# The decay row of a chunk pair through a small transfer and one product of eight rows; no xr where ot stands on GpSimd

## The chip, the cores and the metric

The kernel runs on one core of one Trainium2 chip. Its metric is the device time of an execution in microseconds (us). The core has five engines with an instruction queue each: TensorE (PE; its weight loads are listed apart as PEld), VectorE (DVE), ScalarE (ACT), GpSimd (POOL) and SyncE (SP), which here issues nearly all transfers. An instruction waits, at the head of its engine's queue, for the semaphores of the others.

## The reference

Inputs are `q`, `k`, `v`, `a_re`, `a_im` of shape (4, 8, 768, 48), batch, heads, steps, head width, and the weights of a layer behind. For every batch and head a complex state of 48 x 48 is carried over the steps, and its result goes through a normalised two-layer net:

```python
mag = sqrt(a_re**2 + a_im**2); scale = minimum(mag, 0.999) / (mag + 1e-6)
...
for t in range(S):                  # per batch and head, S complex, 48 x 48
    S = a[t][:, None] * S + outer(k[t], v[t])
    y[t] = q[t] @ real(S)
...
x = y as (B, S, 384)                # heads side by side
mu, var = mean(x), mean((x - mu)**2)
xn = (x - mu) / sqrt(var + 1e-6) * g_ln
out = x + maximum(xn @ w_ch1, 0) @ w_ch2      # 384 -> 1536 -> 384
```

## The kernel before, in words

The 768 steps of a batch are six chunks of 128 steps, taken in pairs: a pair P (0 to 11, three per batch) has the chunks n = 2P and 2P + 1. The recurrence is unrolled inside a pair. With the running product of the decays, written as `e` (magnitude of the product up to a step, `en` its inverse) and `trig` (cosine and sine of its angle), the keys become `ks` and the queries `qs`: the magnitudes go in as `ke = k * en` and `qe = q * e`, the angles as two halves of 64 columns per head, cosine and sine (48 used, the rest is zero padding). Then `am` is the 128 x 128 product of keys and queries per head, `atm` its masked form, `y` the result from `atm` and `v` and from the state `G` of the chunk before, and `gm` the product of `ks` and `v` that is added to the state. At the end of a pair the state is multiplied, row by row, by the magnitude of the decay over the whole pair (L668 and L673, operand `dec`): this is the step that the change is about. Behind `y` come the statistics `bn` (into `mv`, mean and variance), `x`, which is the mean less y, its transposed form `xT`, the net `mm1`, `relu`, `mm2`, and `ot`, the result, which `st` stores.

How the decay over a pair gets to its place: `e` of the pair has steps in partitions and (head, width) along the free axis. Wanted is the last step's row, 8 heads x 48, with the width in partitions and the heads along the free axis. `dps` (L577) does it on TensorE with eight products, one per head: the weights are the 128 x 48 block of `e` of that head, and the moving operand is the last column of the identity, one column wide, so that each product picks out the last row. `decc` (L585) copies the 48 x 8 result from PSUM twice into the tile `dec`, into partitions 0 to 47 and 64 to 111. The tiles `dec` are set to zero at the start by `zdec` (L352). Pairs 2, 5, 8 and 11 are the last of their batch and have no carry, so eight pairs have a `dps`: 0, 1, 3, 4, 6, 7, 9, 10.

How `ot` comes about: it is y + rstd * o, with o from `mm2` in PSUM. `xr` (L708) is -x + mean, which is y again, in 32 bits. On VectorE `ot` is a single operation on o, rstd and xr. GpSimd reads nothing from PSUM in this kernel, so where `ot` stands on GpSimd (chunks 2, 14, 15, 17, 18, 19, 20) ScalarE first writes rstd * o (`oa`, L781), and GpSimd adds xr (L789).

Order: there is no scheduler at build time. A plan written out, the text `PLAN` (L42 to L141), names every step once with its engine (P, A, V, G, S), and for TensorE's results the PSUM bank; on each engine the steps are issued in the order of the text. A step that writes into a tile of a ring (`RINGS`, L25) waits for those that used the tile last. `@name` puts a GpSimd step behind another. SP's queue is one such order too: loads, stores, transposes by transfer (`ksT`, `qsT`, `xT` on S) and the new step all stand in one line, and every transfer uses the next of eight completion semaphores, so that it also waits for the eighth before it. The `warm` steps are products without a use, which run on TensorE while the first loads come in. The weights `w1b` and `w2b` are loaded by GpSimd's own queue (`wl.0`, `wl.1`), `wl.0` behind `qs.0.0.0` on VectorE.

Lines of the profile that come up: L484 `dec` sums ahead of `e`; L488 `e`, `en`; L499 and L503 `ph` (the angles); L521, L532, L544 sine and cosine; L528 `qt`, which turns the angles a quarter; L579 `dps`; L598 transposes of `ks` and `qs`; L621 `am`; L645 `gm`; L682 and L685 `y`; L719 `xtr`, the transposes of x; L752 `mm1`; L776 `mm2`; L764 and L766 `relu`; L806 and L810 `warm`; L448 and L452 loads of a_re and a_im; L400 loads of q, k, v; L370 the small load `gln`; L603 and L725 transposes by transfer; L797 stores. L287, L289 and L292 are helpers that many steps share (copies on ScalarE and VectorE, and products of two tiles).

Of the kernel before, what the change touches and what calls it, by code (L numbers as in the profile page):

```python
# [50 lines left out]
ln.2.0:A car.1.0:V2 q.1.1:S warm.w26:P1 warm.w27:P1 warm.5:P1 warm.6:P1 dec.0.1:P1 lc.0.0:V l.1.0:V en.0.1:A1
warm.7:P4 dec.0.0:P7 e.0.1:A1 iv.2.0:A q.1.0:S lc.1.0:V qe.0.1.0:V warm.w28:P4 warm.w29:P4 warm.8:P4 warm.9:P4
warm.10:P4 dec.1.0:P4 en.0.0:A7 uthc:V vf.0.0:S e.0.0:A7 r.2.0:V e.1.0:A4 warm.11:P1 warm.12:P1 dps.0:P7 are.3.0:S
r2.2.0:V en.1.0:A4 ke.0.0.0:V u.2.0:A gln:S ke.0.1.0:V qe.0.0.0:V aim.3.0:S qe.1.0.1:V qe.1.0.0:V k.1.0:S l.2.0:V
tab.trig.3:A sin.0.0:A6 sin.0.1:A0 warm.w30:P1 warm.w31:P1 warm.w32:P1 warm.w33:P1 warm.13:P1 warm.14:P1@en.1.0
warm.w34:P1 warm.w35:P1 warm.w36:P1 warm.w37:P1 warm.15:P1 warm.16:P1@qe.0.0.0 warm.w38:P1 warm.w39:P1 warm.w40:P1
warm.17:P1 warm.18:P1 warm.19:P1 warm.20:P1 qt.0.0:P6 qs.0.0.1:V sin.1.0:A2 qt.0.1:P0 ks.0.0.1:V vf.1.1:S lc.2.0:V
cos.0.0:A6 ks.0.1.1:V warm.21:P1 warm.22:P1 qt.1.0:P2 qs.1.0.1:V cos.0.1:A0 vf.1.0:S dps.1:P5 qs.0.1.1:V cos.1.0:A2
dec.2.0:P0 ks.0.1.0:V k.2.1:S ks.0.0.0:V decc.0:A7 qs.0.1.0:V kT.0:P6 decc.1:A5 qs.0.0.0:V th.2.0:A qs.1.0.0:V
wl.0:G@qs.0.0.0 qT.0:P2 q.2.1:S v.0:V qT.1:P3 ksT.0:A6 qsT.0:V2 qT.2:P4 ke.1.0.0:G@v.0 k.2.0:S kT.1:P5 qsT.1:A3  # L60
qsT.2:V4 am.0:P6 ke.1.0.1:G@v.0 ksT.1:V5 gm.0:P4 atm.0:V6 ks.1.0.1:G warm.23:P2 warm.24:P2 am.1:P2 qT.3:P5 tab.log.4:A
ln.3.0:A atm.1:V2 y.0:P6 ks.1.0.0:G G.0:A4 e.2.0:A0 warm.w41:P7 warm.25:P7 warm.26:P7 warm.27:P7 gm.1:P4 bn.0:V6
ph.2.0:P2 iv.3.0:A qsT.3:V5 one:G kT.2:P7 x.0:A6 G.1:V4 r.3.0:G en.2.0:A0 ksT.2:V7 warm.28:P5 xtr.0:P6 kT.3:P4 xT.0:V6
am.2:P0 ksT.3:V4 y.1:P5 v.1:G atm.2:V0 am.3:P6 tab.trig.5:A th.3.0:A xr.0:G gm.2:P4 bn.1:V5 ngl:G sin.2.0:A2 r2.3.0:G
ph.3.0:P0 atm.3:V6 x.1:A5 q.2.0:S car.3.0:A0 y.2:P5 G.2:V4 sin.3.0:A0 xtr.1:P7 qt.2.0:P2 are.4.0:S wc.1.1:V gm.3:P4
xT.1:A7 wc.1.0:V qt.3.0:P0 wc.1.2:V cos.2.0:A2 wl.1:G@xT.1 vf.2.0:S wc.0.0:V mm1.0.1.0:P6 wc.0.1:V cos.3.0:A0 bn.2:V5
y.3:P3 aim.4.0:S mm1.0.1.1:P6 wc.0.2:V x.2:A5 wc.2.1:V wc.2.2:V mm1.0.0.1:P0 wc.2.0:V relu.0.1:A6 bn.3:V3
qe.2.0.1:G@wc.2.0 xtr.2:P2 mm1.0.0.0:P0 xT.2:V2 x.3:V3 ke.2.0.1:G@wc.2.0 mm1.0.2.1:P6 gs.3:V4 xtr.3:P2 mm1.0.2.0:P6
rstd.1:G xT.3:V2 tab.log.6:A u.3.0:A ke.2.0.0:V mm1.1.0.1:P2 relu.0.0:A0 l.3.0:V mm1.1.1.0:P4 relu.0.2:A6 mm1.1.1.1:P4
ks.2.0.0:V lc.3.0:V mm1.1.2.1:P0 ks.2.0.1:V relu.1.1:A4 qe.2.0.0:V dec.3.0:P6 rstd.0:A qs.2.0.0:V mm1.1.0.0:P2  # L70
en.3.0:A6 qs.2.0.1:V kT.5:P4 vf.2.1:S e.3.0:A6 qT.4:P5 mm1.1.2.0:P0 ksT.5:A4 qsT.4:V5 qT.5:P6 are.5.0:S G.3:V
relu.1.2:A0 kT.4:P5 qsT.5:V6 mm2.0.0:P4 are.6.0:S ksT.4:V5 ln.4.0:A am.5:P6 mm2.0.1:P4 iv.4.0:A atm.5:V6 aim.5.0:S
mm2.0.2:P4 relu.1.0:A2 am.4:P0 r.4.0:V q.3.0:S mm2.1.0:P5 atm.4:V0 r2.4.0:A v.2:G@r.4.0 mm2.1.1:P5 q.3.1:S mm2.1.2:P5
xr.2:G@r.4.0 u.4.0:A ot.0:V4 mm2.2.0:P6 ln.5.0:A l.4.0:V st.0:S gm.4:P2 mm2.2.1:P6 iv.5.0:A G.4:V2 y.4:P0 lc.4.0:V
ln.6.0:A mm2.2.2:P6 xr.3:V k.3.0:S bn.4:V0 xr.1:G@xr.3 dec.4.0:P2 iv.6.0:A r.5.0:G@xr.3 k.3.1:S x.4:V0 y.5:P1 e.4.0:A2
dps.3:P4 bn.5:V1 xtr.4:P0 vf.3.1:S mm2.3.0:P7 oa.2:A6 xT.4:V0 en.4.0:A2 vf.3.0:S x.5:V1 mm2.3.1:P7 qe.3.0.0:G ot.1:V5
r2.5.0:A xtr.5:P0 k.4.1:S mm2.3.2:P7 rstd.2:G xT.5:V0 qe.3.0.1:V mm1.2.0.0:P0 u.5.0:A aim.6.0:S qs.3.0.0:V
mm1.2.0.1:P0 qs.3.0.1:V q.4.1:S mm1.2.2.1:P2 ke.3.0.0:V ot.3:V7 mm1.2.2.0:P2 k.4.0:S tab.trig.7:A th.4.0:A ke.3.0.1:V
qT.6:P5 relu.2.2:A2 ks.3.0.0:V ph.4.0:P6 q.4.0:S decc.3:V4 ks.3.0.1:V relu.2.0:A0 mm1.2.1.0:P2 l.5.0:V k.5.0:S kT.7:P4
abs.4.0:A6 qsT.6:V5 v.3:G@l.5.0 dps.4:P1 car.4.0:A6 kT.6:P0 vf.4.0:S ksT.7:V4 sin.4.0:A6 r.6.0:G@l.5.0 qT.7:P5  # L80
ksT.6:V0 mm1.2.1.1:P2 are.8.0:S decc.4:A1 qsT.7:V5 th.5.0:A am.6:P6 st.1:S gm.6:P4 relu.2.1:A2 ot.2:G ph.5.0:P0
atm.6:V6 are.7.0:S th.6.0:A ke.4.0.0:G am.7:P2 G.6:V4 y.6:P5 sin.5.0:A0 mm2.5.0:P6 atm.7:V2 ke.4.0.1:G vf.4.1:S
cos.4.0:A mm2.5.1:P6 qe.4.0.1:G bn.6:V5 mm2.5.2:P6 abs.5.0:A0 q.5.0:S ks.4.0.1:V y.7:P2 cos.5.0:A q.5.1:S lc.5.0:V
gm.7:P4 mm2.4.0:P7 ks.4.0.0:V x.6:A5 bn.7:V2 mm2.4.1:P7 xr.5:G@ks.4.0.0 r2.6.0:A aim.7.0:S G.7:V4 qe.4.0.0:G@ks.4.0.0
mm2.4.2:P7 x.7:V2 k.7.0:S dec.5.0:P0 qs.4.0.0:V xtr.6:P2 qs.4.0.1:V xtr.7:P3 st.2:S kT.9:P4 tab.log.8:A e.5.0:A0
# [5 lines left out]
u.7.0:A xr.6:G@qs.5.0.0 vf.5.0:S abs.6.0:V0 r.8.0:G@qs.5.0.0 y.9:P4 y.8:P2 k.6.1:S bn.9:V4 mm2.7.0:P3 q.7.1:S bn.8:V2
gm.9:P7 tab.trig.9:A sin.6.0:A0 mm2.7.1:P3 ke.5.0.1:G gs.9:V7 are.9.0:S x.9:A4 mm2.7.2:P3 ot.6:V6 ke.5.0.0:G th.7.0:A
qT.11:P4 x.8:V2 st.6:S dps.6:P5 G.9:G cos.6.0:A car.6.0:V0 qT.10:P2 q.6.0:S qsT.11:V4 xtr.8:P6 ke.6.0.0:G xtr.9:P7
ph.7.0:P0 xT.8:A6 xT.9:V7 th.8.0:A qsT.10:V2 q.6.1:S mm1.4.1.1:P6 l.7.0:V decc.6:A5 car.7.0:A0 mm1.4.0.1:P4 abs.7.0:A0
ks.5.0.0:V mm1.4.0.0:P4 r2.8.0:V aim.9.0:S sin.7.0:A0 ks.5.0.1:V mm1.4.1.0:P6 relu.4.0:A4 lc.7.0:V kT.10:P1 ot.7:V3
q.7.0:S ke.6.0.1:G@lc.7.0 kT.11:P2 relu.4.1:A6 ksT.10:V1 k.7.1:S mm1.4.2.0:P4 ksT.11:V2 st.5:S am.10:P0 ks.6.0.1:V
am.11:P6 atm.10:V0 dec.7.0:P2 v.5:G@ks.6.0.1 tab.log.10:A rstd.4:A mm1.4.2.1:P4 ln.9.0:A vf.6.0:S xr.8:G@ks.6.0.1
atm.11:V6 y.10:P0 qe.6.0.0:G e.7.0:A2 mm2.9.0:P1 k.8.0:S bn.10:V0 en.7.0:A2 qe.6.0.1:G ph.8.0:P6 q.8.1:S relu.4.2:V4
u.8.0:A ks.6.0.0:G mm2.9.1:P1 are.11.0:S iv.9.0:A gm.10:P2 mm2.9.2:P1 G.10:V2 abs.8.0:A6 mm2.8.0:P3 qs.6.0.0:V x.10:A0
# [747 lines left out]
```

## Time and profile before

| | |
|---|---|
| three runs | 186.82, 187.60, 187.69 us |
| span of the profiled execution | 185.6 us |
| TensorE busy | 177.0 us (95%), 2029 products |
| VectorE, ScalarE, GpSimd busy | 157.7, 154.6, 99.8 us (85, 83, 54%) |
| moved by transfers | 35.34 MB, mean 190 GB/s |
| clock that TensorE was granted | full, mean 1.000 |

The span is the time from the first to the last instruction; the runs' times lie somewhat above it. Busy time is a sum over the whole execution. Where it matters what a step is worth, the place of the step counts: whether the chain of waits, which follows the last instruction back to what released it, runs over its engine there. In a row of the timeline the first number is the start in us from the span's start, the second the length, then engine, line, operation, result and operands. Products on TensorE overlap, so one's length is more than its share of time; the distance from one start to the next is the share. "SPq" marks the issuing of a transfer by SP, not the transfer.

### The profile page before, as it was taken

Reading aid. Unit: us, or ns where it says so; the run is one execution under the profiler, and the core shown is the slowest. Engines: PE = TensorE matmul, PEld = TensorE weight load, DVE = VectorE, ACT = ScalarE, POOL = GpSimd, SP = SyncE. Lnnn points to the kernel's source line nnn. Section 1 sums busy time; section 2 is a strip of 40 time slices with the busy share of each in tenths; the row PEclk is TensorE's granted clock in tenths of the full one; section 3 lists DMA queues with packets and bytes.
Section 4 is the critical chain, followed back from the end, with each engine's and each line's share of the span. In section 5 each row is a group of like instructions: output and inputs, shape, how many; then the busy total and the mean of one; then the engine's idle time right before and its main releaser. Section 6 shows DMA issues by size and latency. Waiting matters only on the chain.

```text
span 185.6 us, 5131 instructions
## 1 busy us (share of the span) xinstructions
PE 177.0 (95%) x2029; PEld 139.0 (75%) x2029; DVE 157.7 (85%) x302; ACT 154.6 (83%) x218; POOL 99.8 (54%) x128
## 2 busy tenths in 40 slices
...
GB/s 154 309 229 206 246 199 191 206 143 189 262 187 213 226 228 230 212 273 181 222 238 151 168 150 241 190 227 200 183 159 139 246 147 202 163 193 73 70 82 87
DMA packets 128440, 35.34 MB, mean 190 GB/s; under 512 B 124448, under 2 KB 127648, under 8 KB 128416
## 3 DMA queue, kind: packets, MB, share of 16 engines
...
q8 instruction: 16, 0.26, 0.6%
...
## 4 chain that ended last, share of the span: by engine, by line
PE 59%; ACT 14%; DMA 10%; DVE 10%; issue 3%; SPq 2%; DVEq 0%
PE banks L752 22%; PE banks L776 19%; DMA w1b<-in_moe_w_ch_dram 7%; PE banks L598 4%; PE banks L621 4%; ACT L815 3%; PE banks L484 2%; DMA are<-in_a_re_dram 2%; DMA k<-in_k_dram 2%; ACT are L457 2%; PE banks L682 2%; DVE l L473 1%; ACT h L764 1%; PE banks L685 1%; ACT w L455 1%
## 5 line engine op out<-in xcount | busy, mean ns | idle before, releaser
L752 PE MATMUL banks<-xT,w1b 128*128 128x256 bf16 x432 | 52.7, 273 | 0.2
L776 PE MATMUL banks<-w2b,h 128*128 128x384 bf16 (+2 forms) x300 | 52.5, 319 | 0.0
L752 PEld LDWEIGHTS <-w1b 128*128 128x128 bf16 x432 | 45.8, 114 | 1.7 <-DVE w1b L381 0.4
L764 ACT ACTIVATE h<-banks 128x1024 bf16<-128x1024 f32 x33 | 32.8, 1022 | 8.3 <-PE banks L752 8.1
L776 PEld LDWEIGHTS <-h 128*128 128x128 bf16 x300 | 26.9, 97 | 14.1
L292 DVE TENSOR_TENSOR atm<-banks,mask 128x1024 bf16<-128x1024 f32 x24 | 28.9, 1218 | 1.9 <-PE banks L621 1.6
L815 ACT ACT_TABLE_LOAD x15 | 19.2, 1283 | 1.0 <-PEq L831 0.8
L292 POOL TENSOR_TENSOR ke<-k,en 128x384 bf16<-128x384 f32 x14 | 12.7, 916 | 8.3 <-DVE l L476 5.6
L292 POOL TENSOR_TENSOR qe<-q,e 128x384 bf16<-128x384 f32 x15 | 13.7, 916 | 6.1 <-DVE w1b L381 1.9
L292 POOL TENSOR_TENSOR ks<-ke,trig 128x768 bf16<-128x768 bf16 x7 | 11.4, 1643 | 6.4 <-PE banks L752 4.2
L621 PE MATMUL banks<-qsT,ksT 128*128 128x128 bf16 x192 | 14.6, 219 | 0.1
L410 POOL TENSOR_SCALAR v<-vf 128x768 bf16<-128x768 f32 x7 | 5.8, 831 | 16.0 <-DVE r L292 8.9
L810 PE MATMUL banks<-u_e 128*128 128x512 f16 x42 | 11.7, 418 | 2.2 <-POOL u_e L320 2.2
L292 POOL TENSOR_TENSOR r<-aim,are 128x768 f16<-128x768 f32 x7 | 12.7, 1817 | 1.9 <-ACT x L699 1.5
L709 POOL TENSOR_SCALAR xr<-x,mv 128x384 f32<-128x384 bf16 x16 | 9.3, 586 | 8.1 <-PE banks L752 3.3
L621 PEld LDWEIGHTS <-ksT 128*128 128x128 bf16 x192 | 12.0, 98 | 1.8 <-DVE ksT L289 0.5
L692 DVE BATCH_NORM_STATS2 stats<-banks 128x6 f32<-128x384 f32 x24 | 13.4, 556 | 0.1
L682 PE MATMUL banks<-v,atm 128*128 128x48 bf16 x192 | 12.1, 183 | 0.3 <-ACT x L699 0.2
L473 DVE SCALAR_TENSOR_TENSOR l<-r,w 128x768 f16<-128x768 f16 (+1 forms) x13 | 11.5, 892 | 0.9 <-ACT r L469 0.7
L791 DVE SCALAR_TENSOR_TENSOR ot<-banks,rstd,xr 128x384 f32<-128x384 f32 (+2 forms) x18 | 10.5, 590 | 2.0 <-PE banks L776 1.6
L455 ACT ACTIVATE w<-are 128x768 f32<-128x768 f32 (+1 forms) x13 | 10.2, 790 | 2.3 <-DMA are<-in_a_re_dram 2.3
L682 PEld LDWEIGHTS <-atm 128*128 128x128 bf16 x192 | 11.0, 96 | 1.2 <-DVE atm L292 0.2
...
## 6 DMA issues: line engine op xcount, KB each, us to landing
k<-in_k_dram SPq DMA_DIRECT2D x24, 192.0 KB, 4.1
q<-in_q_dram SPq DMA_DIRECT2D x24, 192.0 KB, 4.2
vf<-in_v_dram SPq DMA_DIRECT2D x24, 192.0 KB, 4.0
out_dram<-ot SPq DMA_DIRECT2D x23, 192.0 KB, 3.4
are<-in_a_re_dram SPq DMA_DIRECT2D x8, 384.0 KB, 4.7
aim<-in_a_im_dram SPq DMA_DIRECT2D x8, 384.0 KB, 4.8
are<-in_a_re_dram SPq DMA_DIRECT2D x8, 192.0 KB, 3.7
aim<-in_a_im_dram SPq DMA_DIRECT2D x8, 192.0 KB, 3.8
```

The source lines that it names most:

```text
L292: {"DVE": nc.vector, "POOL": nc.gpsimd}[eng(name)].tensor_tensor(**kw)
L455: add(f"ln.{X}", lambda S_=S_: act(out=S_("w"), in_=S_("are"), func=AF.Ln), needs=[f"are.{X}"], uses=[("are", P), ("w", P)])
L473: nc.vector.scalar_tensor_tensor(out=S_("l"), in0=S_("r2"), scalar=0.5, in1=S_("w"), op0=ALU.mult, op1=ALU.add)
L621: nc.tensor.matmul(ps[:, h], lhsT=T("ksT", n)[:, h], rhs=T("qsT", n)[:, h], start=True, stop=True)
L682: nc.tensor.matmul(ps[:, h], lhsT=T("atm", n)[:, h], rhs=T("v", P)[:, c, h], start=True, stop=nfirst)
L692: nc.vector.bn_stats(out=T("stats", n), in_=bank(f"y.{n}")[:, 0:DM])
L752: nc.tensor.matmul(ps[:, jj], lhsT=w1b[:, dc, ts(gi, JG * C)].rearrange("k (p j) -> k j p", j=JG)[:, jj], rhs=T("xT", P)[:, dc].rearrange( ...
L764: act(out=dst, in_=src, func=AF.Relu)
L776: nc.tensor.matmul(bank(f"o.{N}")[:, ws], lhsT=T("h", P)[:, j, ts(c, C)], rhs=w2b[:, j, ws], start=(j == 0), stop=(j == NJ - 1))
L791: nc.vector.scalar_tensor_tensor(out=o, in0=bank(f"o.{N}")[:, ws], scalar=T("rstd", P)[:, ds(c, 1)], in1=xs, op0=ALU.mult, op1=ALU.add)
L810: g.add(f"warm.w{i}", lambda i=i: nc.tensor.matmul(bank(f"warm.w{i}"), lhsT=u_e[:, 0, 0], rhs=u_e.rearrange("p c j t -> p (c j t)"), start ...
L815: g.add(f"tab.{nm}.{i}", lambda tab=tab: nc.scalar.preload_act_table_set(tab))
```

## The change

It does three things. `dps` becomes two steps. `row` is a transfer issued by SP: it takes the last row of `e`, which lies in one partition, and writes its eight stretches of 48 numbers (96 bytes) into eight partitions of a new small tile of 64 columns, whose last 16 columns stay zero (`zrow`, two GpSimd memsets in place of the three of `zdec`). `dps` is then a single product: weights are that tile, 8 rows by 64 columns, the moving operand is the 8 x 8 identity, and the result has 64 rows by 8. `decc` copies 64 rows instead of 48, so that `dec` needs no zeros of its own.

Where `ot` stands on GpSimd, `xr` isn't made any more: `oa` adds the mean along with the scaling, and GpSimd subtracts x. Seven `xr` go, those of chunks 2, 15, 17, 19, 20 on GpSimd and 14, 18 on VectorE.

The plan has the new steps. Every step that stays keeps its engine and its place among the steps of its engine, with two exceptions on TensorE: `dps.0` stands later, behind the warm-up product `warm.w40`, and `dps.10` stands behind `xtr.15` and `ph.10.0`, where it stood ahead of both. The eight `row` steps stand in SP's queue: `row.0` behind `gln`, `row.1` behind `aim.3.0`, `row.3` behind `q.3.0`, `row.4` behind `aim.6.0`, `row.6` behind `q.7.1` and ahead of `are.9.0`, `row.7` behind `are.11.0`, `row.9` behind `q.10.0`, `row.10` behind `k.9.0` and ahead of the transposes `ksT.17` and `qsT.17`. The code for `ke`, `qe`, `ks` and `qs` also gets a form in one operation for both halves; the plan names both halves everywhere, so that form isn't used.

```diff
-            def f_dps():
-                for h in range(H):
-                    nc.tensor.matmul(bank(f"dps.{P}")[0:D, ds(h, 1)],
-                                     lhsT=T("e", P)[:, R - 1, ts(h, D)],
-                                     rhs=ident[:, C - 1:C], start=True, stop=True)
-            add(f"dps.{P}", f_dps, needs=[f"e.{P}.{i}" for i in range(NS)] + ["ident"],
-                uses=[("e", P)], ps=(f"dps.{P}", 1))
-
-            def f_decc():
-                for a in range(2):
-                    put(f"decc.{P}", T("dec", P)[ds(a * HALF, D)], bank(f"dps.{P}")[0:D, 0:H])
-            add(f"decc.{P}", f_decc, needs=[f"dps.{P}", "zdec"], uses=[("dec", P)],
-                ps=(f"dps.{P}", 1))
+            add(f"row.{P}", lambda: nc.sync.dma_start(
+                out=T("row", P)[0:H, 0:D].unsqueeze(1),
+                in_=T("e", P)[C - 1:C, R - 1].rearrange("p (h d) -> p h d", d=D)),
+                needs=[f"e.{P}.{i}" for i in range(NS)] + [f"zrow.{P % RINGS['row']}"],
+                uses=[("e", P), ("row", P)])
+            add(f"dps.{P}", lambda: nc.tensor.matmul(
+                bank(f"dps.{P}")[0:HALF, 0:H], lhsT=T("row", P)[0:H], rhs=ident[0:H, 0:H],
+                start=True, stop=True),
+                needs=[f"row.{P}", "ident"], uses=[("row", P)], ps=(f"dps.{P}", 1))
+            add(f"decc.{P}", lambda: [
+                put(f"decc.{P}", T("dec", P)[ds(a * HALF, HALF)], bank(f"dps.{P}")[0:HALF, 0:H])
+                for a in range(2)],
+                needs=[f"dps.{P}"], uses=[("dec", P)], ps=(f"dps.{P}", 1))
...
-    g.add("zdec", lambda: [nc.gpsimd.memset(t, 0.0) for t in tiles["dec"]], needs=["ue"])
+    for i in range(RINGS["row"]):
+        g.add(f"zrow.{i}", lambda i=i: nc.gpsimd.memset(tiles["row"][i][0:H], 0.0), needs=["ue"])
...
-                add(f"oa.{N}", lambda n=n, N=N, ws=ws, c=c: nc.scalar.mul(
-                    out=T("ot", n)[:, ws], in_=bank(f"o.{N}")[:, ws], mul=T("rstd", P)[:, ds(c, 1)]),
+                add(f"oa.{N}", lambda n=n, N=N, ws=ws, c=c: act(
+                    out=T("ot", n)[:, ws], in_=bank(f"o.{N}")[:, ws], func=AF.Identity,
+                    scale=T("rstd", P)[:, ds(c, 1)], bias=T("mv", P)[:, c, 0:1]),
...
-                        nc.gpsimd.tensor_tensor(out=o, in0=o, in1=xs, op=ALU.add)
+                        nc.gpsimd.tensor_tensor(out=o, in0=o, in1=T("x", n)[:, ws], op=ALU.subtract)
```

More of the change, by code (lines that the diff above doesn't have):

```diff
@@ L51 @@
[L51 to L85, printed above, removed]
@@ L91 @@
[L91 to L99, printed above, removed]
-xr.9:V y.11:P2 qs.6.0.1:V mm2.8.1:P3 bn.11:V2 qsT.13:S r.9.0:G@qs.6.0.1 xtr.10:P0 mm2.8.2:P3 x.11:V2 tab.trig.11:A
@@ L141 @@
-mm2.24.2:P2 st.23:S ot.24:V2 st.24:S
+ue:G are.1.0:S are.0.0:S are.0.1:S uth:V aim.1.0:S warm.w0:P0 pad.qs.1:G warm.w1:P0 aim.0.0:S pad.ks.2:G warm.w2:P0
+ident:G aim.0.1:S warm.w3:P0 car0.0:G are.2.0:S warm.w4:P0 pad.qs.2:G tab.log.0:A ln.1.0:A warm.w5:P0 uec:G warm.w6:P0
+iv.1.0:A k.0.0:S qrow:G warm.w7:P0 zrow.0:G@uth zrow.1:G warm.w8:P0 car0.1:G@uth ln.0.0:A warm.w9:P0 pick:G@uth
+ln.0.1:A q.0.1:S warm.w10:P0 iv.0.1:A r.1.0:V warm.w11:P0 pad.qs.0:G iv.0.0:A warm.w12:P0 q.0.0:S warm.w13:P0
+warm.w14:P0 r.0.1:V warm.w15:P0 warm.w16:P0 r.0.0:V warm.w17:P0 warm.w18:P0 tab.trig.1:A th.1.0:A vf.0.1:S r2.0.1:V
@@ new lines @@
+warm.10:P4 qe.0.1.0:V are.3.0:S dec.1.0:P4 uthc:V en.0.0:A7 r.2.0:V warm.11:P1 e.0.0:A7 warm.12:P1 gln:S e.1.0:A4
+row.0:S aim.3.0:S warm.w30:P1 r2.2.0:V warm.w31:P1 en.1.0:A4 warm.w32:P1 row.1:S ke.0.0.0:V warm.w33:P1 k.1.0:S
+warm.13:P1 u.2.0:A ke.0.1.0:V warm.14:P1@en.1.0 warm.w34:P1 warm.w35:P1 qe.0.0.0:V vf.1.1:S warm.w36:P1 warm.w37:P1
+qe.1.0.1:V warm.15:P1 warm.16:P1@qe.0.0.0 warm.w38:P1 qe.1.0.0:V warm.w39:P1 vf.1.0:S warm.w40:P1 l.2.0:V dps.0:P7
+warm.17:P1 warm.18:P1 tab.trig.3:A sin.0.0:A6 warm.19:P1 warm.20:P1 sin.0.1:A0 k.2.1:S qt.0.0:P6 qs.0.0.1:V sin.1.0:A2
@@ new lines @@
+qt.0.1:P0 ks.0.0.1:V lc.2.0:V warm.21:P1 warm.22:P1 ks.0.1.1:V cos.0.0:A6 qt.1.0:P2 qs.1.0.1:V cos.0.1:A0 dps.1:P5
+qs.0.1.1:V cos.1.0:A2 q.2.1:S ks.0.1.0:V dec.2.0:P0 ks.0.0.0:V qs.0.1.0:V decc.0:A7 kT.0:P6 decc.1:A5 qs.0.0.0:V
+k.2.0:S th.2.0:A qs.1.0.0:V qT.0:P2 v.0:V q.2.0:S qT.1:P3 ksT.0:A6 wl.0:G@qs.0.0.0 qsT.0:V2 qT.2:P4 are.4.0:S kT.1:P5
+qsT.1:A3 qsT.2:V4 ke.1.0.0:G@v.0 am.0:P6 vf.2.0:S ksT.1:V5 gm.0:P4 ke.1.0.1:G@v.0 warm.23:P2 warm.24:P2 atm.0:V6
+am.1:P2 ks.1.0.1:G qT.3:P5 tab.log.4:A ln.3.0:A aim.4.0:S atm.1:V2 y.0:P6 warm.w41:P7 warm.25:P7 G.0:A4 warm.26:P7
@@ new lines @@
+warm.27:P7 e.2.0:A0 ks.1.0.0:G gm.1:P4 bn.0:V6 ph.2.0:P2 iv.3.0:A qsT.3:V5 x.0:A6 G.1:V4 one:G r.3.0:G kT.2:P7
+en.2.0:A0 warm.28:P5 xtr.0:P6 ksT.2:V7 kT.3:P4 xT.0:V6 am.2:P0 ksT.3:V4 v.1:G y.1:P5 atm.2:V0 tab.trig.5:A th.3.0:A
+am.3:P6 xr.0:G gm.2:P4 sin.2.0:A2 ngl:G r2.3.0:G bn.1:V5 ph.3.0:P0 vf.2.1:S atm.3:V6 x.1:A5 car.3.0:A0 y.2:P5
+sin.3.0:A0 G.2:V4 xtr.1:P7 qt.2.0:P2 wc.1.1:V gm.3:P4 xT.1:A7 qt.3.0:P0 wc.1.0:V cos.2.0:A2 wc.1.2:V are.5.0:S
+wc.0.0:V mm1.0.1.0:P6 wc.0.1:V cos.3.0:A0 wl.1:G@xT.1 bn.2:V5 y.3:P3 are.6.0:S mm1.0.1.1:P6 wc.0.2:V x.2:A5 wc.2.1:V
@@ new lines @@
+qe.3.0.1:V mm1.2.0.0:P0 u.5.0:A qs.3.0.0:V mm1.2.0.1:P0 q.4.0:S qs.3.0.1:V mm1.2.2.1:P2 ke.3.0.0:V ot.3:V7 k.5.0:S
+mm1.2.2.0:P2 tab.trig.7:A th.4.0:A ke.3.0.1:V qT.6:P5 vf.4.0:S ks.3.0.0:V relu.2.2:A2 ph.4.0:P6 decc.3:V4 ks.3.0.1:V
+relu.2.0:A0 l.5.0:V mm1.2.1.0:P2 are.8.0:S abs.4.0:A6 kT.7:P4 qsT.6:V5 v.3:G@l.5.0 dps.4:P1 kT.6:P0 car.4.0:A6
+ksT.7:V4 st.1:S sin.4.0:A6 r.6.0:G@l.5.0 are.7.0:S qT.7:P5 ksT.6:V0 mm1.2.1.1:P2 vf.4.1:S decc.4:A1 qsT.7:V5 th.5.0:A
+am.6:P6 q.5.0:S gm.6:P4 relu.2.1:A2 atm.6:V6 ot.2:G ph.5.0:P0 th.6.0:A ke.4.0.0:G q.5.1:S am.7:P2 G.6:V4 y.6:P5
@@ new lines @@
+mm2.7.1:P3 ke.5.0.1:G gs.9:V7 x.9:A4 mm2.7.2:P3 ot.6:V6 ke.5.0.0:G th.7.0:A qT.11:P4 x.8:V2 st.6:S dps.6:P5 G.9:G
+cos.6.0:A q.6.0:S car.6.0:V0 qT.10:P2 q.6.1:S qsT.11:V4 xtr.8:P6 ke.6.0.0:G xtr.9:P7 aim.9.0:S ph.7.0:P0 xT.8:A6
+xT.9:V7 th.8.0:A qsT.10:V2 mm1.4.1.1:P6 l.7.0:V decc.6:A5 car.7.0:A0 mm1.4.0.1:P4 q.7.0:S abs.7.0:A0 ks.5.0.0:V
+mm1.4.0.0:P4 r2.8.0:V sin.7.0:A0 k.7.1:S ks.5.0.1:V mm1.4.1.0:P6 relu.4.0:A4 lc.7.0:V st.5:S kT.10:P1 ot.7:V3
+ke.6.0.1:G@lc.7.0 vf.6.0:S kT.11:P2 relu.4.1:A6 ksT.10:V1 k.8.0:S mm1.4.2.0:P4 ksT.11:V2 am.10:P0 q.8.1:S ks.6.0.1:V
```

153 lines of the change are left out of this document (91 added, 62 removed), and 2 rows, old and new, of the table RINGS.

## The prediction

> **What bounds the kernel now.** I read first the busy time of each engine in five stretches, cut where the chain of waits changes its engine (columns: the stretch, its length, busy time and count of each engine, clock, DMA share, GB/s).
>
> ```profile
> 37.50:82.00 44.50, 44.46 (x513) 36.88 (x514) 42.10 (x85) 43.10 (x57) 21.80 (x24) 1.00 1.00 217
> 82.00:117.00 35.00, 35.00 (x432) 28.09 (x429) 33.55 (x61) 34.21 (x52) 24.56 (x27) 1.00 0.95 195
> 117.00:182.10 65.10, 64.86 (x771) 53.99 (x769) 52.95 (x100) 43.35 (x60) 34.64 (x40) 1.00 0.76 160
> ```
>
> From 37.5 to 182.1 us TensorE (first pair of numbers) has next to no idle time, at full clock. What it issues there sets the end: a product less is time won, and a wait put in front of a product is time lost, because nothing behind it is idle that could take it up. Before 37.5 the chain runs over ScalarE, VectorE and the load of w1b. GpSimd (last) is busy for half the time or a little more. The transfers are the second full thing: the DMA engines are busy for 100, 95 and 76% of the three stretches, nearly all of it with SP's one queue.
>
> The chain of waits in order of time (start, length, what) shows what the eight products of a `dps` cost:
>
> ```profile
> 126.43 0.20 PE banks L645 x8
> ...
> 129.03 0.17 PE banks L719 x3
> 129.20 0.29 PE banks L579 x8
> 129.49 0.27 PE banks L719 x3
> ```
>
> Eight products of 48 columns with full 128x128 weights (L645) take 0.20, so 25 ns each. The eight of one column (L579) take 0.29, and the three transposes behind them 0.27, where the same three ahead took 0.17. So 0.09 and 0.10 us go into passing from 128x128 weights to 128x48 ones and back, whatever number of products stands between.
>
> **The change part by part.** The profiled execution spans 185.6 us; the three runs have 186.82 to 187.69, median 187.6. I work on the span and add the 2.0 us between it and the median (1.2 to 2.1 over the three runs).
>
> *Seven products fewer per pair.* 7 x 25 ns = 0.175 us. The two switches stay if 8 rows by 64 columns are as partial as 128x48; I take that. If they vanished, nearly the whole 0.29 + 0.10 would go, less one product: 0.36. Of the eight `dps`, the first two start at 17.1 and 22.5 us, where the chain doesn't run over TensorE: worth 0. The one at 117.0 ends in a wait for another engine (timeline; in brackets idle time and releaser):
>
> ```profile
> 117.02 0.36 PE L579 MATMUL banks<-ident,e 128*48 128x1 bf16 x8
> 117.09 0.35 DVE L289 COPY xT<-banks 128x384 bf16<-128x384 bf16 x1
> 117.49 0.58 PEld L752 LDWEIGHTS <-w1b 128*128 128x128 bf16 x6 [0.20 <-DVE xT L289]
> ```
>
> A shorter `dps.7` only makes that wait longer: 0. Five remain (`dps.3`, 4, 6, 9, 10): 0.88 us, between 0.88 and 5 x 0.36 = 1.8.
>
> [...]
>
> *Eight new transfers in SP's queue.* Each `row` is one instruction on SP, 8 pieces of 96 bytes. Does SP stand still for it? `row.6` is issued behind `q.7.1`, `row.9` and `row.10` around `k.9.0`:
>
> ```profile
> 82.72 0.83 ACT L488 ACTIVATE e<-banks 128x768 bf16<-128x768 f32 x1
> 124.97 1.50 ACT L488 ACTIVATE e<-banks 128x768 bf16<-128x768 f32 x2
> ...
> 84.25 1.30 SPq L400 DMA_DIRECT2D q<-in_q_dram  x1
> 85.66 2.22 SPq L452 DMA_DIRECT2D are<-in_a_re_dram  x2
> 126.91 1.23 SPq L400 DMA_DIRECT2D q<-in_q_dram  x1
> 128.18 0.58 SPq L400 DMA_DIRECT2D k<-in_k_dram  x1
> 128.87 2.02 SPq L603 DMA_TRANSPOSE ksT<-ks  x1
> ```
>
> `e.6` is ready at 83.55, SP gets to the row at 85.6; `e.9` and `e.10` at 126.47, SP at 128.14. No wait on SP. The issue itself costs some 0.5 us (aim's row below), most of it while the queue is full anyway; behind it wait loads of later pairs, which aren't awaited at once. I count 0, at most 8 x 0.5 us on SP alone.
>
> What is late next is `dps`, which now waits for the landing. How long does a small transfer take? First three issues on SP, then times from issue to landing (last column), the first six each from a window of one issue: are, gln, aim at these times, q at 84.25, k at 128.18, ksT at 128.87; the last from the page.
>
> ```profile
> 16.26 0.84 SPq L448 DMA_DIRECT2D are<-in_a_re_dram  x1
> 17.14 0.80 SPq L370 DMA_DIRECT2D gln<-in_moe_g_ln_dram  x1
> 17.98 0.49 SPq L448 DMA_DIRECT2D aim<-in_a_im_dram  x1
> ...
> are<-in_a_re_dram SPq DMA_DIRECT2D x1, 384.0 KB, 4.3
> gln<-in_moe_g_ln_dram SPq DMA_DIRECT2D x1, 1.5 KB, 3.5
> aim<-in_a_im_dram SPq DMA_DIRECT2D x1, 384.0 KB, 5.1
> ...
> q<-in_q_dram SPq DMA_DIRECT2D x1, 192.0 KB, 4.5
> k<-in_k_dram SPq DMA_DIRECT2D x1, 192.0 KB, 3.6
> ksT<-ks SPq DMA_TRANSPOSE x1, 4.0
> ...
> out_dram<-ot SPq DMA_DIRECT2D x1, 64.0 KB, 1.5
> ```
>
> gln moves 1.5 KB and still takes 3.5 us: it lands at 20.6, about 0.1 behind the 384 KB issued ahead of it (16.26 + 4.3). A small transfer stands in line. So I let a row land 0.1 us behind the load ahead of it. Bounds: 1.5 us after issue, as the small store with nothing ahead of it at the end of the page's list, and the landing of the transfer behind it.
>
> [...]
>
> `row.3`, 4, 7 and 9 have time. The tightest is `row.4`, behind `aim.6` on SP:
>
> ```profile
> 58.31 0.87 SPq L448 DMA_DIRECT2D aim<-in_a_im_dram  x1
> ...
> 65.21 0.29 PE banks L579 x8
> ```
>
> It is issued at 59.2 and wanted at 65.2; even the longest of the times above, 5.1, fits: 0. The two that count:
>
> `row.6` lands at 84.25 + 4.5 + 0.1 = 88.85 (bounds 87.1 and 89.4). On TensorE (timeline):
>
> ```profile
> 88.42 0.36 PE L579 MATMUL banks<-ident,e 128*48 128x1 bf16 x8
> 88.71 0.62 PE L598 MATMUL banks<-ident,qs 128*128 128x128 bf16 x8
> ...
> 129.13 0.36 PE L579 MATMUL banks<-ident,e 128*48 128x1 bf16 x8
> 129.42 0.34 PE L719 MATMUL banks<-ident,x 128*128 128x128 bf16 x3
> 130.09 0.49 PE L503 MATMUL banks<-th,u_thc 128*128 128x384 f16 x2
> 130.41 0.61 PE L598 MATMUL banks<-ident,qs 128*128 128x128 bf16 x8
> ```
>
> With `dps.3` and `dps.4` shorter TensorE is there at 88.42 - 0.35 = 88.07, waits 0.78, and the next transposes start at 88.85 + (0.29 - 0.175) = 88.97, against 88.71: 0.26 late in place of 0.53 early.
>
> `row.10` lands at 128.18 + 3.6 + 0.1 = 131.88 (bounds 129.1 + 1.5 = 130.6, and ksT's 132.87). `dps.10` is moved behind `ph.10`, which buys time: without the eight products and their switches in front, `ph.10`'s last product starts at 130.25 - 0.39 = 129.86, and `dps.10` is due 0.16 + 0.09 later, at 130.11, with the 0.26 at 130.37. It waits 1.5 us. The transposes of `qT.16` then start at 131.88 + 0.12 = 132.0, against 130.41: 1.59 late. Behind them stand `mm1.7`, `am` and everything else on TensorE; only `dps.9` gives 0.175 back.
>
> *`row.0` and `row.1`.* The rows of TensorE, ScalarE and of the chain:
>
> ```profile
> 20.37 0.60 PE L806 MATMUL banks<-u_e 128*128 128x256 f16 x4
> ...
> 21.96 1.60 ACT L532 ACTIVATE trig<-banks 128x384 bf16<-128x384 int16 x3
> ...
> 24.53 12.18 DMA w1b<-in_moe_w_ch_dram
> ```
>
> `row.0` is issued at 17.98, behind gln, and lands at about 20.8; `dps.0` is due ahead of the four products of L806, at 20.37 less the 0.39 of the old `dps.0`: 20.0. `row.1` stands behind aim (17.98 + 5.1 = 23.1), and `dps.1` was at 22.5. Both waits, near 0.8, fall where TensorE isn't the chain: 0, at most 0.5 if `cos` and so the VectorE products ahead of w1b's load are held up.
>
> *The rest.* Seven `xr` go, five on GpSimd at 586 ns and two on VectorE at 413, none of them in the chain; the GpSimd `ot` subtracts x instead of adding xr; `oa` adds a bias, as the ScalarE x of L699 does; the copies of `decc` have 64 rows for 48; `zrow` replaces `zdec`, GpSimd memsets of 0.1 us. All 0: TensorE covers them, and without that cover the seven would be worth 3.8 us of their engines.
>
> ```profile
> L709 POOL TENSOR_SCALAR xr<-x,mv x16: 576/586/592, 33.4 to 175.2; 128x384 f32<-128x384 bf16 x16
> L709 DVE TENSOR_SCALAR xr<-x,mv x8: 410/413/415, 55.6 to 179.3; 128x384 f32<-128x384 bf16 x8
> ```
>
> *Sum.* Once `dps.10` waits, what happened before is forgotten but for the queue's own time: +1.59 - 0.175 = +1.4 us. Span 187.0, time 189.0.
>
> **The rivals.**
>
> [...]
>
> *The rows are all in time* (faster). The 0.88 us are won whole: 186.7, with the switches gone too 185.8. It needs `row.10` on the spot by 129.8, 0.7 us after its issue, or SP two us earlier; the shortest time in the list is 1.5.
>
> *The start slips too* (slower still). `row.0` holds back `dps.0`, the four products behind it and `qt.0.0`, which feeds `cos` on ScalarE; with `row.1` and SP's extra issues w1b and the queue come 0.5 to 1.0 later: 189.5 to 190.0. Against it: ScalarE starts `cos` (L532) only at 21.96, when `qt.0.0`, at 20.85 + 0.12 + 4 x 0.11 = 21.4, is through, and w1b's load waits for VectorE at 24.53, not for TensorE.
>
> **How the numbers follow.** Forecast 0.52, the start slips 0.14, not in line 0.21, all in time 0.13. A change of 0.5% is what a measurement here can tell: below 186.66 faster, above 188.54 slower. The forecast and the late start are slower (0.66), the case not in line is within (0.21), all in time is taken as faster (0.13). The forecast's own range, by `row.10` up to ksT's landing and 0.5 us of queue either way, is 188.3 to 190.2. The range of 187.0 to 190.2 takes in the case not in line and leaves out all in time (0.13) and a little above.
>
> **What would show it.** `dps` with one product of 64x8, TensorE idle 0.5 to 1 us before the sixth pair's and 1 to 2 before the tenth's, released by the row's DMA; rows of 2.5 to 3.5 us to landing; ScalarE's `e` never what SP waits for. [...]

## The result, and the profile after

Twenty runs of the changed kernel have a median of 189.38 us (187.57 to 192.37), the kernel before beside them 187.75; the ratio, which leaves out the slow runs, five of the changed kernel (190.98 us and more) among them, is 1.0064, 95% interval 1.0037 to 1.0092. That is +1.2 us, 0.7 to 1.7; the forecast was +1.4, a time of 189.0 us. The profiled execution spans 187.3 us, where 187.0 was forecast and 185.6 stood before.

The same three stretches as in the prediction, now of the changed kernel (length, then busy time and count of each engine, TensorE first; the last stretch is longer, since TensorE ends later):

```profile
37.50:82.00 44.50, 44.50 (x502) 36.79 (x502) 41.83 (x84) 43.39 (x58) 21.02 (x24) 1.00 1.01 218
82.00:117.00 35.00, 33.97 (x414) 27.28 (x412) 32.71 (x59) 33.34 (x49) 24.17 (x25) 1.00 0.93 191
117.00:184.20 67.20, 65.19 (x762) 53.77 (x757) 53.38 (x99) 44.66 (x61) 31.98 (x37) 1.00 0.78 156
```

TensorE had next to no gap in all three; now it is idle for 1.0 us of the second and 2.0 of the third. The waits of TensorE (who waits for whom: us in all, times, longest) and its timeline at the two places say for what:

```profile
PE banks L599 <- DMA row<-e: 2.7, 2, 1.6
```

```profile
87.54 0.61 PE L615 MATMUL banks<-ident,qs 128*128 128x128 bf16 x8
89.18 0.19 PE L599 MATMUL banks<-ident,row 8*64 8x8 bf16 x1 [1.03 <-DMA row<-e]
89.30 0.62 PE L615 MATMUL banks<-ident,qs 128*128 128x128 bf16 x8
...
130.28 0.49 PE L509 MATMUL banks<-th,u_thc 128*128 128x384 f16 x2
132.39 0.19 PE L599 MATMUL banks<-ident,row 8*64 8x8 bf16 x1 [1.62 <-DMA row<-e]
132.51 0.62 PE L615 MATMUL banks<-ident,qs 128*128 128x128 bf16 x8
```

These are `dps.6` and `dps.10`, the two that the prediction named. The transposes behind them start at 89.30 and 132.51, against 88.71 and 130.41 before: 0.59 and 2.10 us late. SP's issues around the two rows, and the time from issue to landing of the load that stands directly ahead of each (last column, from a window of that issue alone):

```profile
83.92 0.70 SPq L406 DMA_DIRECT2D q<-in_q_dram  x1
84.73 0.69 SPq L594 DMA_DIRECT2D row<-e  x1
...
127.31 0.43 SPq L406 DMA_DIRECT2D q<-in_q_dram  x1
127.85 0.68 SPq L594 DMA_DIRECT2D row<-e  x1
128.58 0.44 SPq L406 DMA_DIRECT2D k<-in_k_dram  x1
129.12 0.66 SPq L594 DMA_DIRECT2D row<-e  x1
...
q<-in_q_dram SPq DMA_DIRECT2D x1, 192.0 KB, 5.0
...
k<-in_k_dram SPq DMA_DIRECT2D x1, 192.0 KB, 3.8
```

`q.7.1` lands at 83.92 + 5.0 = 88.9 and the product that needs the row starts at 89.18; `k.9.0` lands at 128.58 + 3.8 = 132.4 and the product starts at 132.39. The 0.8 KB of a row were complete with the load ahead, 4.4 and 3.2 us after their own issue.

Not the whole row stood in line, though. The trace has the steps of the semaphore that tells of a landing. For a row there are nine: one 1.1 to 1.5 us after the issue, then eight, which I take for its eight pieces, and the product starts 0.05 us behind the last. Of `row.6`, seven of the eight are there by 87.20, 2.5 us after the issue, and the last at 89.14; of `row.10`, five by 131.35 and three from 132.27 to 132.34. TensorE waited for the slowest pieces. The eight rows of this execution took 2.3 to 4.4 us from issue to the last step; six of them ended within 0.25 us of the landing of the bulk load ahead, `row.3` and `row.7` 0.8 and 0.6 us before it.

### The profile page after: what moved, and what is told of

Its sections match the earlier page's. It is cut to its first block, busy times and chain, and to the rows that moved or that the text cites. A ratio compares the mean times of both kernels' runs of the same rounds, so it can differ in the third digit from the quotient of the medians.

```text
span 187.3 us, 5017 instructions
## 1 busy us (share of the span) xinstructions
PE 176.7 (94%) x1973; PEld 137.8 (74%) x1973; DVE 157.4 (84%) x300; ACT 155.2 (83%) x218; POOL 95.9 (51%) x122
## 4 chain that ended last, share of the span: by engine, by line
PE 61%; DVE 9%; DMA 8%; SPq 8%; ACT 7%; POOL 3%; issue 3%; DVEq 0%; POOLq 0%; ACTq 0%
PE banks L769 21%; PE banks L793 19%; PE banks L615 6%; SPq L406 5%; DMA row<-e 4%; PE banks L638 4%; DMA aim<-in_a_im_dram 2%; PE banks L490 2%; DMA are<-in_a_re_dram 2%; PE banks L699 2%; POOL ks L297 2%; PE banks L509 2%; PE banks L702 2%; PE banks L736 1%; DVE l L479 1%
## 5 line engine op out<-in xcount | busy, mean ns | idle before, releaser
L828 PE MATMUL banks<-u_e 128*128 128x512 f16 x42 | 12.7, 444 | 2.2 <-POOL u_e L325 2.2
L294 DVE COPY qsT<-banks 128x1024 bf16<-128x1024 bf16 x16 | 10.8, 683 | 2.3 <-PE banks L615 2.2
L798 ACT ACTIVATE ot<-banks,mv,rstd 128x384 f32<-128x384 f32 x7 | 4.7, 670 | 9.4 <-DMA out_dram<-ot 5.7
```

The source lines that it names most:

```text
L294: nc.vector.tensor_copy(out=dst, in_=src)
L828: g.add(f"warm.w{i}", lambda i=i: nc.tensor.matmul(bank(f"warm.w{i}"), lhsT=u_e[:, 0, 0], rhs=u_e.rearrange("p c j t -> p (c j t)"), start ...
```

## The experiments

Each was run twelve times, beside the kernel before. The runs of before had medians of 187.26, 187.37 and 187.30 us in the three sets of four; each set had another chip, so that kernels of different sets are best compared by their ratios to before.

**xr_alone.** The kernel before with the xr part only: no `xr` where `ot` is on GpSimd, `oa` adds the mean, GpSimd subtracts x. The eight products stay.

```diff
-nc.gpsimd.tensor_tensor(out=o, in0=o, in1=xs, op=ALU.add)
+nc.gpsimd.tensor_tensor(out=o, in0=o, in1=T("x", n)[:, ws], op=ALU.subtract)
```

> Only the second part of the change, on the kernel before: no xr for the seven chunks whose ot stands on GpSimd, oa adds the mean, GpSimd subtracts x; dps stays eight products. Theory (the loss is the two waits for row.6 and row.10, and TensorE covers everything else): ratio to before 1.000, between 0.997 and 1.003; TensorE has no new idle time. Rival (part of the 1.2 to 1.7 us comes from this part, since oa now takes 670 ns in place of 579 on ScalarE and GpSimd's ot waits for it): ratio 1.003 to 1.006.

187.12 us (186.94 to 188.22), ratio 0.9971 (0.9942 to 0.9999), span 185.4. The xr part isn't where the loss comes from. That it helps is hardly separable from nothing, though `oa` takes 0.67 us with the mean and 0.58 without.

**row_on_act.** The changed kernel with `row.6` and `row.10` issued by ScalarE, right behind their `e`.

```diff
-... row.6:S ... row.10:S ...
+... e.6.0:A4 row.6:A ... e.10.0:A6 row.10:A ...
```

> The changed kernel, with row.6 and row.10 issued by ScalarE right behind their e instead of by SP; dps.6 and dps.10 stay where they are. Theory (a row stands in line behind the loads that SP has issued): on a queue of its own the row lands within 2.5 us of its issue, row.6 near 86.5 and row.10 near 129.5, TensorE's waits of 1.1 and 1.8 us for them go; ratio to before 0.995 to 1.000, since ScalarE gives up to 0.7 us twice for issuing. Rival (the line is at the transfer engines themselves, whichever queue the row comes by): rows take 3 to 4.5 us as from SP, row.6 lands at 87.5 to 88, row.10 at 130 to 131, the wait at dps.6 nearly goes because the issue is a microsecond earlier, that at dps.10 shrinks to below 1 us; ratio 1.000 to 1.004.

188.85 us (188.15 to 190.4), ratio 1.008 (1.0045 to 1.0115): no better. ScalarE's timeline, then TensorE's:

```profile
83.77 1.20 ACTq L594 DMA_DIRECT2D row<-e  x1
...
88.61 0.57 ACT L716 ACTIVATE x<-banks,mv 128x384 bf16<-128x384 f32 x1
...
127.69 0.66 ACTq L594 DMA_DIRECT2D row<-e  x1
...
130.53 0.84 ACT L498 ACTIVATE th<-r 128x768 f16<-128x768 f16 x1
```

```profile
89.24 0.61 PE L615 MATMUL banks<-ident,qs 128*128 128x128 bf16 x8 [1.10 <-ACT x L716]
89.78 0.19 PE L599 MATMUL banks<-ident,row 8*64 8x8 bf16 x1
...
131.42 0.32 PE L509 MATMUL banks<-th,u_thc 128*128 128x384 f16 x1 [0.70 <-ACT th L498]
```

The row products no longer wait. But issuing a row holds ScalarE for 1.20 and 0.66 us. The `x` and `th` behind it start at 88.61 and 130.53, where the changed kernel had them at 86.77 and 129.06 (0.45 and 0.6 of that is there ahead of the issue, at `e`), and TensorE waits for these: 1.10 and 0.70. The wait has changed its place and its releaser, and much of its size is still there. Nor did the row come within the 2.5 us of the theory: by the last step of its semaphore `row.6` took 2.65 us (from SP 4.40), `row.10` 3.37 (from SP 3.22), landing at 131.06 where the rival had 130 to 131. So the line isn't SP's queue alone.

**late_dps10, late_both, late_both_again.** The product is asked for later: `dps.10` behind the fourth of the six groups of `mm1.7`, and in late_both `dps.6` behind the fifth of `mm1.4` as well; `decc` behind them, in other banks.

```diff
-... dps.10:P4 qe.9.0.1:G ... mm1.7.2.0:P6 ...
+... mm1.7.2.0:P6 dps.10:P5 th.11.0:A ... atm.16:V2 decc.10:V5 ...
-... dps.6:P5 G.9:G ... mm1.4.2.0:P4 ...
+... mm1.4.2.0:P4 dps.6:P3 decc.6:A3 ...
```

> The changed kernel with dps.10 and its copy moved behind mm1.7.2.0 and atm.16, some 3.5 us later on TensorE and into PSUM bank 5; nothing else. Theory: the wait for row.10 goes (1.8 us in the profile of after), that for row.6 stays at 1.1 us, so the time is 1.4 to 1.8 us below the changed kernel: ratio to before 0.999 to 1.003. Rival (the wait is only a sign of a later bottleneck, the transfers being as late for everything else): TensorE waits elsewhere behind it and the ratio stays above 1.004.

> As the run before, and dps.6 with its copy moved behind mm1.4.2.0 too, some 6 us later, into bank 3. Theory: no wait for a row after 37.5 us; the five shorter products give 0.88 us: span 184.7 to 185.0 where before has 185.6, ratio 0.994 to 0.998. Rival (the saving of the products is swallowed by ScalarE and VectorE between 82 and 117 us, where they are nearly as full as TensorE): ratio 0.998 to 1.001, with idle time of TensorE at xT or l there.

late_dps10: 187.98 us (186.13 to 190.68), ratio 0.9992 (0.9954 to 1.0029), as the theory has it: without the wait at `dps.10` the change is neither a loss nor a gain. late_both: 188.30 us (187.14 to 191.07), ratio 1.0014 (0.9979 to 1.005), where the theory had 0.994 to 0.998. The second wait goes and nothing more is won. TensorE's waits in late_dps10:

```profile
PE banks L599 <- DMA row<-e: 2.0, 2, 1.2
...
PE banks L769 <- ACT xT L292: 0.9, 1, 0.9
```

One of the two row waits is `dps.6`; the other, 0.84 us, is `dps.0` in the start, which did not wait in the changed kernel's own profile. And a wait that no trace above has: 0.87 us before `mm1.9` at 155 us. late_both has the same two kinds. So I had two suspects for the missing 0.9 us, the start's rows and this wait.

**start_products, late_start_products.** Pairs 0 and 1 get the eight products back, in the changed kernel (start_products) and in late_both (late_start_products). late_both_again is late_both run once more in the same set.

```diff
+        if P < 2:
+            def f_dps():
...
-        if not last:
+        elif not last:
             add(f"row.{P}", ...
```

> The changed kernel with pairs 0 and 1 alone put back to the eight products (no row.0, no row.1; dps.0 at its old place on TensorE); dps.6 and dps.10 stay where they wait. Theory, that the two rows of the start cost TensorE a gap whose length differs from run to run, and that a long gap there costs clock as well: the long times go (none of 190 or more, granted clock at 0.996 or above in every run), while the middle of the runs falls by 0.3 to 1.2 us below the changed kernel's 189.38: 188.2 to 189.1, ratio 1.005 to 1.009 in the middle, since the 2.5 us before dps.6 and dps.10 are still there. Rival, that the start costs nothing: times and clocks spread as in the changed kernel, up to 192 us and down to 0.99.

> All three causes taken away: dps.6 behind mm1.4.2.0, dps.10 behind mm1.7.2.0, and pairs 0 and 1 by eight products. Theory: five pairs at 0.17 us less each is 0.86 us, and the xr part gave 0 to 0.5 in its own run, with nothing on the other side: 0.9 to 1.4 us faster, ratio 0.9925 to 0.996, no run of 190 or more, and no wait of TensorE on a row left. Rival, that the start costs nothing: no better than late_both, ratio 1.001.

> late_both again, beside the others on one chip, so that the price of the start's two rows is a difference within one set of runs. Theory: 0.8 to 2 us above late_start_products in the middle, with some runs at a clock of about 0.99 and 189 us or more, and in each profile a wait on row.0 or row.1. Rival: equal to late_start_products to within 0.3 us.

start_products: 189.95 us (187.23 to 192.53), ratio 1.0073 (1.0037 to 1.0109). The theory falls here: the long times stay with the start's rows gone, so they don't need those rows. The ratio is what the theory had for the middle of the runs, as the waits at `dps.6` and `dps.10` are left. late_start_products: 187.71 us (186.74 to 189.91), ratio 1.0007 (0.9984 to 1.0031); late_both_again: 188.25 us (186.39 to 191.45), ratio 1.0027 (1.0000 to 1.0054). The start's rows may cost the 0.5 us between the medians, but the intervals overlap; the 0.8 to 2 us expected aren't there. In the profiles they delay the first `mm1` from 37.28 to 38.04.

late_start_products has no wait on a row at all and still gains nothing. ScalarE in it, first two rows, and in the kernel before, last two:

```profile
152.44 0.83 ACT L415 CAST v<-vf 128x768 bf16<-128x768 f32 x1 [2.00 <-DMA vf<-in_v_dram]
...
153.88 0.47 ACT L292 COPY xT<-banks 128x384 bf16<-128x384 bf16 x1
```

```profile
150.79 0.84 ACT L408 CAST v<-vf 128x768 bf16<-128x768 f32 x1
...
152.21 0.50 ACT L287 COPY xT<-banks 128x384 bf16<-128x384 bf16 x1
```

`v.10` stands ahead of `e.11` and `xT.19` on ScalarE and waits 2.00 us for its load; `xT.19` comes at 153.88 instead of 152.21, and `mm1.9` waits for it. Before, the load had just arrived, at 150.69. This wait differs from execution to execution: in that of late_both_again, the kernel of late_both once more, `v.10` waits 0.69 us and TensorE doesn't stand before `mm1.9`.

**late_full_weights.** late_start_products with the row tile cleared and used in full, so that the weights are 128x128 like those of the neighbours.

```diff
-lhsT=T("row", P)[0:H], rhs=ident[0:H, 0:H]
+lhsT=T("row", P), rhs=ident[:, 0:H]
```

> As late_start_products, with the row tile cleared and loaded over all 128 rows and columns, so that the product's weights and rows are 128 by 128 like those of its neighbours. Theory, by the prediction's term of 0.09 us into the small form and 0.10 out of it: the step from the product before to the one behind it falls from 0.23 to about 0.05 us, 0.75 to 0.95 us in five pairs, ratio 0.988 to 0.992. Rival, that the two gaps belong to the change of bank or to the waits and not to the small form: as late_start_products to within 0.2 us.

TensorE around `dps.6`, in late_start_products and in late_full_weights:

```profile
93.47 0.82 PE L784 MATMUL banks<-xT,w1b 128*128 128x256 bf16 x6
94.22 0.19 PE L614 MATMUL banks<-ident,row 8*64 8x8 bf16 x1
94.34 1.07 PE L653 MATMUL banks<-qsT,ksT 128*128 128x128 bf16 x16
```

```profile
94.35 0.82 PE L784 MATMUL banks<-xT,w1b 128*128 128x256 bf16 x6
95.01 0.17 PE L614 MATMUL banks<-ident,row 128*128 128x8 bf16 x1
95.03 1.11 PE L653 MATMUL banks<-qsT,ksT 128*128 128x128 bf16 x16
```

From the small product to the next 0.12 becomes 0.02 us; from the last product ahead to the first behind, 0.323 becomes 0.138. The 0.185 us is the prediction's 0.09 + 0.10, and it goes away with the form, here and at `dps.4`, `dps.9` and `dps.10`; at `dps.3` the step only goes from 0.233 to 0.224. The time doesn't follow: 188.06 us (186.99 to 189.24), ratio 1.0031 (1.0007 to 1.0055).

**late_v_behind, late_full_v.** The two kernels just told of, with `v.10` moved behind `xT.19` on ScalarE.

```diff
-... v.10:A ke.11.0.1:V ... e.11.0:A4 ... xT.19:A1 ...
+... e.11.0:A4 ... xT.19:A1 v.10:A ...
```

> late_start_products with one step moved: v.10 behind xT.19 on ScalarE, so that the wait for the load vf.10 no longer stands ahead of e.11 and xT.19. Theory, that this wait is what ended TensorE's 0.80 us gap at 153.6 us: the gap goes, 0.5 to 0.8 us below late_start_products (187.71), 186.9 to 187.2 us, ratio 0.996 to 0.999. Rival, that another late step takes its place, xT.18's transposing transfer first of all, which landed at 153.3 us there: less than 0.3 us of change.

> late_v_behind with the weights of the row product at 128 by 128 (late_full_weights with v.10 moved). Theory: the steps around the product stay at 0.08 to 0.14 us, 0.19 less in five pairs, and without the wait at 154 us the 0.9 us shows in the end: 186.0 to 186.4 us, ratio 0.991 to 0.995. Rival, that what TensorE gains is waited for again at a load or a transfer further on: equal to late_v_behind to within 0.3 us.

late_v_behind: 187.38 us (186.78 to 188.67), ratio 0.9991 (0.9962 to 1.0021). The gap before `mm1.9` is gone from its profile, but the time fell by 0.33 only, across two sets. late_full_v: 186.95 us (186.25 to 189.21), ratio 0.9969 (0.9939 to 0.9998), another 0.43 instead of 0.9. Both lie between theory and rival.

**no_rows, rows_unused.** The changed kernel's order and xr part with the eight products in all pairs: without any row transfer, and with all eight issued on SP and read by nobody.

```diff
-add(f"dps.{P}", lambda: nc.tensor.matmul(bank(f"dps.{P}")[0:HALF, 0:H], lhsT=T("row", P)[0:H], ...
+add(f"dps.{P}", f_dps, needs=[f"e.{P}.{i}" for i in range(NS)] + ["ident"], ...
```

> The changed kernel's order and its xr part, with the eight products in all pairs and no row transfer at all. Theory, that whatever is lost comes with the row transfers and the waits on them: as the kernel before with the xr part alone, ratio 0.996 to 1.000, times as narrow as there (up to about 188.5 us). Rival, that the new order of the other steps costs: ratio 1.003 or more, or times up to 190 us and more.

> As no_rows, with the eight row transfers issued on SP at the changed kernel's places and nothing reading them: what the transfers cost by themselves, without any wait on them. Theory, that SP's 0.67 us for each issue and their packets push later loads back until an engine waits for one (as ScalarE did for vf.10 in late_start_products): 0.3 to 1.2 us above no_rows, and times that spread further. Rival, that the transfers are free as long as nobody waits for them: equal to no_rows to within 0.2 us.

no_rows: 187.16 us (186.69 to 190.62), ratio 0.9981 (0.9953 to 1.0008), span 184.9; eleven of its twelve runs lie below 188.4. rows_unused: 186.24 us (186.07 to 187.02), ratio 0.9939 (0.9912 to 0.9966). Neither has a wait on a row. First no_rows' largest wait of TensorE behind the warm-up, then from rows_unused the row issues (min, median, max in ns) and the one larger wait behind the warm-up:

```profile
PE banks L503 <- DVE atm L296: 0.3, 1, 0.3
```

```profile
L595 SPq DMA_DIRECT2D row<-e x8: 657/684/1381, 19.0 to 128.2; - x8
...
PE banks L799 <- DMA w2b<-in_moe_w_ch_dram: 0.6, 1, 0.6
```

The theory that the transfers by themselves push later loads back falls: with the same eight issues of 0.68 us on SP the kernel isn't slower. It is 0.9 us faster than no_rows, which neither side expected; the two intervals just overlap. The profiles explain part of it. From 20 us on TensorE's products start at the same times in both, within 0.1 us, up to the wait for w2b at 49.0 us, and from there to the end rows_unused is 0.67 us later. But from the last product to the end of the span no_rows takes 3.6 us and rows_unused 3.1, and all of this lies behind the landing of the last store (1.6 and 1.1 us from there to the end). So 0.5 us is won in the closing of the kernel, where no product and no load of data is left; why, is open. The profiled execution of rows_unused, 186.81 us, is one of its five longer ones; how the other seven, 186.07 to 186.24, went isn't on record. rows_unused leaves out nothing of the work and is the fastest kernel of this study, faster than the kernel before, and by the ratios than the changed one.

## Why the prediction was right

*TensorE as the bound, and the two places.* Right. Between no_rows and the changed kernel, which differ in who fetches the row and in the place of `dps.0`, the last product ends at 181.3 and 184.2 us, 2.9 apart, and TensorE's two new gaps are 1.03 + 1.62 us. By the ratios to before the two are 1.6 us apart: the profiled execution of no_rows, 186.69 us, is the fastest of its twelve.

*Seven products fewer, 0.175 us a pair.* Right as a local price: from the product ahead to the product behind, the trace has 0.405 and then 0.233 at `dps.3`, 0.441 and 0.269 at `dps.4`, 0.494 and 0.324 at `dps.9`: 0.17 each. `dps.7`, priced at nothing, goes from 0.623 to 0.620. The two switches stayed, and late_full_weights showed that they belong to the small form: 0.185 us for the change and back at `dps.6`.

*Five pairs, 0.88 us.* This term was too large as a gain for the whole, which the sum hid because it let `dps.10` forget what came before. Look behind `dps.3`: TensorE's three transposes of the next x and VectorE's `x` that they need, in no_rows (first three rows) and in the changed kernel:

```profile
57.12 0.34 PE L734 MATMUL banks<-ident,x 128*128 128x128 bf16 x3
57.88 0.61 DVE L717 TENSOR_SCALAR x<-banks,mv 128x384 bf16<-128x384 f32 x1
58.60 0.33 PE L734 MATMUL banks<-ident,x 128*128 128x128 bf16 x3
```

```profile
57.13 0.34 PE L736 MATMUL banks<-ident,x 128*128 128x128 bf16 x3
58.06 0.61 DVE L719 TENSOR_SCALAR x<-banks,mv 128x384 bf16<-128x384 f32 x1
58.73 0.34 PE L736 MATMUL banks<-ident,x 128*128 128x128 bf16 x3
```

From one group of transposes to the next 1.48 us becomes 1.60, because VectorE's `x` ends at 58.67: of 0.17 won, 0.11 is handed back 1.5 us later. At `dps.4` 0.08 comes back at the transposes right behind it and 0.09 more 1.1 us later, so that nothing is left. For the other pairs only the sum was followed: at 150 us, with all five savings behind it and no wait on a row, TensorE in late_start_products is 0.25 us behind its place in no_rows, not 0.86 ahead. This fits that late_start_products and late_v_behind come out at the time of no_rows or above: TensorE is full, but the others are so close behind it that a product less is no time less. That rests on one execution of each.

*A row stands in line.* Right in its size for these two, and the term that decided; as a mechanism it holds for the slowest pieces (one of eight at `row.6`, three at `row.10`), not for the whole row. The landing was forecast 0.1 us behind the load ahead; the products start 0.3 and 0.0 us behind it. The size was off by what lay in front: `row.10` was read at 132.39 instead of 131.88, of which 0.4 is SP, which reached `k.9.0` at 128.58 instead of 128.18. SP was 0.4 late at `q.10.0` already (127.31 against 126.91); the 0.68 us of `row.9` behind it cost nothing more, since `q.10.0` held SP for 0.43 us in place of 1.23. The sum had SP on time, and only the range had 0.5 us of queue either way. Another 0.2 is the load itself, 3.8 instead of 3.6. `row.6` was 0.3 later than forecast, since `q.7.1` took 5.0 us and not 4.5. So `qT.16` was 2.10 us late, not 1.59.

*The sum.* +2.10 at `qT.16`, -0.17 at `dps.9`, -0.19 ahead of `mm1` at 132.8, which no_rows has too, so that it isn't the rows', and +0.41 at two later places make 2.15: the last product ends at 184.2 us instead of 182.0. Forecast were 1.4. The rows of the last products, before and then in the changed kernel:

```profile
177.91 4.09 PE L776 MATMUL banks<-w2b,h 128*128 128x384 bf16 x36
```

```profile
180.11 4.09 PE L793 MATMUL banks<-w2b,h 128*128 128x384 bf16 x36
```

The span grew by 1.7 only, since from the last product to the end 3.1 us pass instead of 3.6. This is no chance of one execution: it is 3.6 in the profiles of all three kernels without row transfers (before, xr_alone, no_rows) and 3.1 in all five with the eight rows on SP. The forecast had no such term. So TensorE's delay came out half as long again as forecast, the end of the kernel gave 0.5 us back, and that the time lies so near the forecast is in part luck.

*The start, counted at nothing, 0.5 at most.* Right in the changed kernel's profile, where neither `dps.0` nor `dps.1` waits and the first `mm1` starts at 37.45 against 37.48. In the four other profiles with the start's rows read, TensorE waited 0.66 to 1.07 us for `row.0`, and `mm1` began at 37.80, 37.88, 38.04 and 40.11. So that rival is real in some executions. Its price between the medians of late_both_again and late_start_products, 0.5 us, isn't separated from zero.

*xr.* Right: nothing, or a gain that is small (0.2 us in the span, 0.5 by the ratio of xr_alone, whose interval nearly reaches 1).

*The rivals.* "Not in line", to which the chances give 0.21, is that a row lands without waiting for the load ahead. It fell: `row.10` was issued at 129.12 and read 3.27 us later, with that load, though five of its eight pieces were there after 2.2. None of the eight rows in the changed kernel's profile was whole under 2.3 us after its issue. "All in time" fell with the gaps; where the product was put late enough that it was in time, the 0.88 us did not appear either.
